# One attention kernel on one core: the two o visits of a burst, run per half of the query columns

## The chip, the cores and the metric

The kernel runs on one core of one Trainium2 chip. The metric is the device time of one execution in microseconds (us), the median of three runs; lower is better. Engines are named as the profile names them: PE is TensorE's matmuls, PEld its weight loads, DVE is VectorE, ACT is ScalarE, POOL is GpSimd, SP is the queue that issues the DMAs. A bank is one of the eight PSUM banks, 512 fp32 columns on 128 partitions.

## The reference

```
x = A_x                                          # 1 x 2048 x 640
g = sigmoid((x * gate_w).sum(-1, keepdims=True))
q = x @ wq  (32 heads of 20)   k = x @ wk   v = x @ wv   (one k and v for all heads)
a = softmax(q k^T * 20 ** -0.5) v @ wo
h = layernorm(B_x)                               # 1 x 2048 x 640
b = (w2^T gelu(w1^T h + b1) + b2)                # the MLP runs over the 2048 tokens, 1728 hidden
out = g * a + (1 - g) * b
```

Attention over 2048 queries and keys for 32 heads, an MLP over the token axis, and a gate that mixes the two.

## The kernel before, in words

The attention is cut into 32 blocks `n` (4 blocks of 512 queries by 8 groups of 4 heads), and each block into 16 units of 128 keys: 512 units. Four kinds of work meet on TensorE, and from about 190 us on they are interleaved in 248 **stretches** of one form (the loop `for j in range(n_st)`):

- **S** (L689, in `qk`): scores of one head for 128 keys by 512 queries, into a bank of 512 columns. ACT reads the bank, takes the exponential and writes a tile `p` (L701); here and there one ACT instruction serves two neighbouring banks (1024 columns).
- **M** (L507, in `ms_next`): the same scores the other way round, only for the row maxima of later blocks. DVE reduces the bank (L515).
- **F** (L839 in the MLP2 stretches; L1014 and L967 before and after them): a step of the MLP or of the output projection, 320 columns, accumulated in a bank `g` of its own.
- **o visits** (L724, in `pv_mm`): `p` times `v` for the four heads of a unit, four fp32 matmuls with 32 output rows each, side by side in the four column groups of the array. Each such matmul is two records in the trace, each with a weight load.

S, M and F matmuls use one half of the array's rows each (62, 60 or 64 rows), so two lanes run at a time: one lane holds the stretch's eight S and some M, the other holds F with an M at its start and one or more at its end. A stretch ends with a **burst**: the o visits of two units, eight matmuls over all 128 rows, accumulated into one bank. After the burst `collect` lets ACT copy the bank to SBUF (L742 for the first pair of units of a block, into `osum`; L745 for the other pairs, into `part`), and POOL adds `part` to `osum` (L746).

S, M and bursts share seven banks (the eighth is `g`). The order of all instructions is fixed while the program is built, by a planner that keeps its own estimate of when each bank is free (`free`), when ACT and DVE are done (`clock`) and how far each lane is (`lane`). A new matmul takes the bank that the planner expects to be free first (`next_free`), and waits on the chip for the engine that last read that bank (`touch`). So a burst waits for a bank, as an S or an M does.

The stretches differ by the F work in them. Those with more than 22 F steps are the MLP's first layer (MLP1, 72 stretches), those with 15 belong to the output projection (48), and the 128 between them are the second layer, **MLP2**. In MLP2 each output tile half has 41 F steps in one lane half and 40 in the other, cut into two batches each, so that of four stretches in a row three have 20 F steps and one has 21. The MLP2 stretches run from about 613.5 to 1330.2 us.

Names and lines of the steps: `burst` holds `next_free`, the call of `pv_mm` for both units and `collect`; L724 is the burst's matmul, L742 and L745 its copy, L746 the sum on POOL, L701 the exponential, L515 the reduction.

Of the kernel before, what the change touches and what calls it, by code (L numbers as in the profile page):

```python
# [10 lines left out]
F32 = mybir.dt.float32  # L11
F32R = mybir.dt.float32r
AF = mybir.ActivationFunctionType
# [5 lines left out]
P = 128  # L19
S, D, H, DH, F = 2048, 640, 32, 20, 1728  # L20
NS = S // P
# [4 lines left out]
NB = 512  # L26
# [13 lines left out]
def mix_kernel(ctx: ExitStack, tc: tile.TileContext, A_x, A_wq, A_wk, A_wv, A_wo,  # L40
               B_x, B_w1, B_b1, B_w2, B_b2, gate_w, out):
    nc = tc.nc
    x = A_x[0]
    y_out = out[0]

    def f32(ap):
        return ap.bitcast(F32)
# [12 lines left out]
    v_sb = const.tile([P, NS, 32], F32, name="v_sb")  # L60
# [392 lines left out]
    p_all = pp_pool.tile([P, 16 * NB], F32, name="p")  # L453
    ev = ctx.enter_context(tc.tile_pool(name="ev", bufs=1))
    copies = ctx.enter_context(tc.tile_pool(name="copies", bufs=2))
    sums = ctx.enter_context(tc.tile_pool(name="sums", bufs=2))
# [8 lines left out]
    def touch(ins, reads=(), writes=(), also=()):  # L465
        need = list(also)
        for r in reads:
            need.append(writer[r])
            readers.setdefault(r, []).append(ins)
        for w in writes:  # L470
            need += readers.pop(w, [])
            writer[w] = ins
        for n in {n.ins.name: n for n in need}.values():
            tc.add_manual_dep(ins.ins, n.ins.name, SYNC, reason="a bank or a p region used again")
        me = str(ins.ins.engine)
        engines.add(me)
        for e in engines - {me}:
            tc.declare_no_dep(ins.ins, group=e, keep=[n.ins for n in need], reason="other banks and p regions")
        tc.add_to_no_dep_group(me, ins.ins)

    def bank(i):
        return span(i, 1) if i < 7 else xs[2]

    def span(i, n):
        t, at = (xs[0], i) if i < 3 else (xs[1], i - 3)
        return t[:, at * NB:(at + n) * NB]
# [121 lines left out]
    with tc.tile_pool(name="psb", bufs=2, space=PSUM, side="right") as psb, \  # L608
# [4 lines left out]
        at, skip, last = 0, 3, NS * PRO - 6  # L613
# [8 lines left out]
        for fc in range(PRO):  # L622
            pu = [psb.tile([P, NB], F32, name=f"pu{r}") for r in range(2)]
            for hf in range(4):
# [4 lines left out]
                for c in range(HS):  # L629
                    st = hf * HS + c  # L630
                    for k, (w, h) in enumerate(((wh, h_hi[0]), (wh, h_lo[0]), (wl, h_hi[0]))):
                        for r in range(2):
                            rows = slice(64 * r, 64 * r + 64)
                            nc.tensor.matmul(pu[r][:, :HD2], w[rows, c, :], h[rows, st, :],  # L634
                                             start=(st == 0 and k == 0), stop=(st == NS - 1 and k == 2))
# [42 lines left out]
    units = [(n, kb) for n in range(NU) for kb in range(NS)]  # L678
    ptiles = {}
    last = {"half": None, "ins": None, "sig": None}  # L680
    flag = const.tile([1, 1], F32, name="flag")

    p_free, p_left = list(range(4)), {}
# [32 lines left out]
    osum = {}  # L716
    later = []

    arrived = []

    def pv_mm(u, o, first, last, i):
        for hh in range(4):
            j = ptiles.pop((u, hh))
            mm = nc.tensor.matmul(o[32 * hh:32 * hh + 32, :], v_sb[:, units[u][1], :], p_all[:, j * NB:(j + 1) * NB],  # L724
                                  start=first, stop=last, skip_group_check=True)
            touch(mm, [("p", j)], [("x", i)], [arrived.pop(0)] if arrived else [])
            p_left[j // 4] -= 1
            if not p_left[j // 4]:
                p_free.append(j // 4)

    def put_o(n, t):
        qb, g = divmod(n, NQ)
        for j in range(2):
            for hh in range(4):
                r = (4 * g + hh) * DH
                nc.sync.dma_start(out=o_scr[j, r:r + DH, qb * NB:(qb + 1) * NB], in_=f32(t[j][32 * hh:32 * hh + DH, :]))

    def collect(u, o, i):
        n, kb = units[u]
        if kb == 1:  # L740
            osum[n] = sums.tile([P, NB], F32, name="osum")
            touch(nc.scalar.activation(osum[n], o, AF.Copy), [("x", i)])  # L742
        else:
            part = copies.tile([P, NB], F32, name="part")
            touch(nc.scalar.activation(part, o, AF.Copy), [("x", i)])  # L745
            nc.gpsimd.tensor_add(osum[n], osum[n], part)  # L746
        if kb == NS - 1:
            later.extend(norm_steps(n))

    def norm_steps(n):  # L750
        t = osum[n]
        ls = ev.tile([P, NB // 32], F32, name="ls")
        rb = ev.tile([P, NB], F32, name="rb")
        hi, lo = rb.bitcast(F32R), t.bitcast(F32R)

        def rows_out():
            nc.sync.dma_start(out=l_scr[n], in_=t.rearrange("(h r) q -> h r q", r=32)[:, DH, :])

        def rows_in():
            nc.sync.dma_start(out=ls, in_=l_scr[n].rearrange("h (c e) -> (h c) e", e=NB // 32))  # L760

        def inverse():
            nc.vector.reciprocal(ls, ls)

        def inverse_out():
            nc.sync.dma_start(out=r_scr[n].rearrange("h (c e) -> (h c) e", e=NB // 32), in_=ls)

        def inverse_in():
            for hh in range(4):
                nc.sync.dma_start(out=rb[32 * hh:32 * hh + 32, :], in_=r_scr[n][hh:hh + 1, :].to_broadcast([32, NB]))  # L770

        def scale():
            nc.gpsimd.tensor_mul(t, t, rb)

        def split():
            nc.gpsimd.tensor_copy(hi, t)
            nc.gpsimd.tensor_sub(lo, t, f32(hi))

        return rows_out, rows_in, inverse, inverse_out, inverse_in, scale, split, lambda: put_o(n, (hi, lo))
# [269 lines left out]
    ph = [(rows[1 - b], rest if b else [], done if b else []) for rows, rest, done in seq for b in range(2)]  # L1049
# [24 lines left out]
    X_US, F_US, O_US = 0.2345, 0.1468, 0.869  # L1074
    W_US, FIRST_US, LAST_US, NEXT_US, SEEN_US = 0.11, 0.1, 0.333, 0.13, 0.43
# [3 lines left out]
    lane, fresh, free = [0.0, 0.0], [True, True], [0.0] * 3 + [1.3] * 4  # L1079
    state = {"at": 0.0, "f": 0.0, "last": 0.0}  # L1080
    reduces = []

    def spend(e, us, at=0.0):
        clock[e] = max(clock[e], at) + us
        return clock[e]

    def next_free():
        return min(range(len(free)), key=lambda i: free[i])
# [99 lines left out]
        while reduces:  # L1188
            reduces.pop(0)[2]()

    def burst(us):
        i = next_free()
        t = max(max(lane) + FIRST_US, state["last"] + LAST_US, free[i]) + len(us) * O_US
        o = bank(i)
        if len(wants) > us[1] // 2 + 2:
            counts = share(us[1] // 2 + 2)
            n = max((given[b] + counts[b] - 1) // 32 for b in range(2))
            if n in qtiles:
                arrived.extend(q_loads.pop(n, ()))
        for u in us:  # L1200
            pv_mm(u, o, u == us[0], u == us[-1], i)
            fetch_at(u)
        collect(us[-1], o, i)
        each, hold = EACH["act"]
        free[i] = spend("act", each, t + 0.25) - each + hold
        lane[:] = [t + NEXT_US] * 2
        fresh[:] = [True, True]

# [8 lines left out]
    def fetch_at(u):  # L1217
        n, kb = units[u]
        if kb == 11 and n + 1 < NU:
            fetch_max(n + 1)  # L1220
# [7 lines left out]
    at = m + 2 * 2 * 2 * NS  # L1228
    left, n = 64 * NU - sum(given) - sum(wants[:at]), n_st - 3 - at
# [12 lines left out]
    for j in range(n_st):  # L1242
        h, i = j % 2, j // 2
        due, stores[:] = stores[:], []
        blocks = [], []
        ss = [lambda at, u=u, pr=pr: qk(u, pr, h, at, blocks[u % 4 // 2], pairs.get(2 * (u % 4) + pr, 1))
              for u in range(4 * i, 4 * i + 4) for pr in range(2)]
        fs, rest, done = ph[j]
        counts, before = share(j), sum(given)
        ms = [[f for f in (ms_next(x) for _ in range(counts[x])) if f] for x in (h, 1 - h)]  # L1250
        owed = sum(counts) - (sum(given) - before)
        pop_chain()
        arrange(h, ss, *ms, fs, done)
        if j % 8 == 7:
            u = j // 8
            for n in (u + 3, u + 4) if u == 0 else (u + 4, u + 5) if u == 1 else (u + 5,):
                if n != 29:
                    new_q(n)
        for f in due:
            f()  # L1260
        if follow:
            follow.pop(0)()
            if len(row_max) == NU and follow:
                follow.pop(0)()
                stores.pop()()
        if not follow and not (j + 1 < n_st and len(ph[j + 1][0]) == 20):
            n = len(row_max)
            follow += ms_done()
            if follow:
                follow.pop(0)()  # L1270
                follow.append(lambda n=n: store_max(n))
        settle()
        pop_chain()
        w1_load(fetched[0] + 3)
        for f in rest:
            f()
        spend("dve", 0.03)
        spend("act", 0.1)
        if j == 8 * 25 - 1:
            new_q(29)  # L1280
        if j:
            burst((2 * j - 2, 2 * j - 1))
        if j == n_st - 2:
            raw = last_wo()

# [146 lines left out]
    for st, d in held:  # L1432
        oT, _ = room(st)
        for j, w in ((0, wo_hi), (1, wo_hi), (0, wo_lo)):
            a, new = acc_at(st, d)
            touch(nc.tensor.matmul(bank(a)[:, :HD2], oT[:, j, 3, :], w[:, 3, d * HD2:(d + 1) * HD2],
                                   start=new, stop=False), writes=[("x", a)])
# [33 lines left out]
```

## Time and profile before

| what | before |
|---|---|
| three timed runs | 1611.63, 1611.82, 1612.45 us; median 1611.82 us |
| profiled execution | span 1610.9 us, the only time that the page gives of it; 0.9 us below the median of the runs |
| PE, PEld | 1602.7 us (99%), 1118.5 us (69%) |
| DVE, ACT, POOL | 1379.7 us (86%), 1261.7 us (78%), 845.4 us (52%) |
| granted TensorE clock | 1.000 of full speed over the span |
| copy of a burst, L745 | 216 of 128x512, mean 601 ns |
| o matmuls, L724 | 4096 records, mean 598 ns |

How to read it: a row of a group gives line, engine, operation, the tile that is written and the one that is read, its shape, how often it ran, the busy time and the mean of one in ns, and then the engine's idle time just before these instructions and who ended it. In a timeline each row is a run of like instructions, with its start, the time from its first start to its last end, and a count; idle time before it and the releaser stand in brackets. A matmul's end is modelled, and matmuls overlap, so a PE that is busy all the time can still be waiting: starts tell more than busy time.

### The profile page before, as it was taken

How to read it: one execution, taken by the hardware profiler on the slowest of the kernel's cores; microseconds unless marked ns; L12 is line 12 of the kernel's file. 1: busy time of each engine (PE TensorE's matmuls, PEld its weight loads, DVE VectorE, ACT ScalarE, POOL GpSimd, SP SyncE). 2: the span in 40 equal slices, each digit the busy share in tenths (PEclk: the TensorE clock that was granted, in tenths of full speed). 3: DMA queues.
4: the chain of work that ended last, by engine and by line, in shares of the span. 5: the costliest groups of instructions: out<-in, count | busy, mean ns of one | idle time of the engine just before them, and what ended most of it. 6: DMA issues, size and time to landing. Idle time of an engine off the chain costs nothing.

```text
span 1610.9 us, 39433 instructions
## 1 busy us (share of the span) xinstructions
PE 1602.7 (99%) x14859; PEld 1118.5 (69%) x14859; DVE 1379.7 (86%) x2626; ACT 1261.7 (78%) x2353; POOL 845.4 (52%) x930
## 2 busy tenths in 40 slices
PE   9999999999999999999999999999999999999998
PEld 7899867767767766666666666666666666666665
DVE  6689899999999999888988989888898986667743
ACT  4445677778778778888888888888888889999996
POOL 6567767777777776544554344444444333333340
PEclk9999999999999999999999999999999999999999
DMA  7665322222222122222211121122211113322341
GB/s 214 205 172 139 93 60 71 65 75 76 69 69 75 49 75 63 81 69 69 59 56 58 38 61 57 54 60 61 61 55 48 46 48 98 118 84 82 89 137 58
DMA packets 180437, 129.53 MB, mean 80 GB/s; under 512 B 41617, under 2 KB 150062, under 8 KB 180246
## 3 DMA queue, kind: packets, MB, share of 16 engines
q1 hardware_dynamic: 179958, 126.68, 27.7%
q8 instruction: 117, 1.92, 0.5%
q14 instruction: 74, 0.61, 0.1%
q10 hardware_dynamic: 288, 0.33, 0.1%
HBM read 93.57 MB, written 32.15 MB: 78 GB/s over the span
## 4 chain that ended last, share of the span: by engine, by line
PE 98%; DMA 1%; DVE 0%; POOL 0%; issue 0%; SPq 0%; ACT 0%; DVEq 0%; POOLq 0%
PE xs L724 30%; PE xs L689 18%; PE xs L507 18%; PE g L839 11%; PE g L1014 7%; PE pu L634 4%; PE pp L303 3%; PE g L967 3%; PE xs L921 1%; PE pp L367 0%; PE x L507 0%; DMA xa<-in_A_x_dram 0%; DMA q_scr<-ql 0%; PE g L507 0%; PE pt L295 0%; PE pp L192 0%
## 5 line engine op out<-in xcount | busy, mean ns | idle before, releaser
L515 DVE TENSOR_REDUCE mp<-xs 128x1 f32<-128x512 f32 x1946 | 1197.9, 684 | 146.5 <-PE xs L689 77.5
L701 ACT ACTIVATE p<-xs 128x512 f32<-128x512 f32 (+1 forms) x1841 | 1014.9, 682 | 3.5 <-PE xs L689 3.4
L746 POOL TENSOR_TENSOR osum<-osum,part 128x512 f32<-128x512 f32 x216 | 279.4, 1294 | 615.3 <-ACT part L745 602.7
L724 PE MATMUL xs<-p,v_sb 128*32 128x512 f32 x4096 | 492.3, 598 | 0.0
L689 PE MATMUL xs<-q,kst 62*128 62x512 f32 x1344 | 477.2, 418 | 1.3 <-ACT p L701 1.3
L507 PE MATMUL xs<-kst,q 60*128 60x512 f32 x1242 | 433.1, 416 | 0.0
L689 PEld LDWEIGHTS xs<-q,kst 62*128 62x128 f32 x1344 | 236.8, 185 | 74.3 <-DVE mp L515 53.9
L745 ACT ACTIVATE part<-xs 128x512 f32<-128x512 f32 x216 | 129.9, 601 | 199.7 <-PE xs L724 198.4
L1014 PE MATMUL g<-slot,w 64*128 64x320 f32 x1728 | 266.8, 306 | 0.0
L724 PEld LDWEIGHTS xs<-p,v_sb 128*32 128x32 f32 x4096 | 107.1, 109 | 226.6 <-issue 157.4
L1014 PEld LDWEIGHTS g<-slot,w 64*128 64x128 f32 x1728 | 259.1, 184 | 2.0
L507 PEld LDWEIGHTS xs<-kst,q 60*128 60x128 f32 x1242 | 207.3, 185 | 72.4 <-DVE mp L515 52.0
L127 POOL TENSOR_TENSOR w<-wr,w 128x512 fp32r<-128x512 f32 (+1 forms) x180 | 225.8, 1256 | 34.3 <-ACT w L124 18.6
L689 PE MATMUL xs<-slot,kst 62*128 62x512 f32 x569 | 207.6, 418 | 0.0
L507 PE MATMUL xs<-kst,slot 60*128 60x512 f32 x576 | 204.2, 418 | 0.0
L839 PE MATMUL g<-u,w 64*128 64x320 f32 x1296 | 201.7, 306 | 0.0
L839 PE MATMUL g<-slot,w 64*128 64x320 f32 x1296 | 201.4, 306 | 0.0
L839 PEld LDWEIGHTS g<-u,w 64*128 64x128 f32 x1296 | 195.7, 184 | 1.7
L839 PEld LDWEIGHTS g<-slot,w 64*128 64x128 f32 x1296 | 195.6, 184 | 1.5
L689 PEld LDWEIGHTS xs<-slot,kst 62*128 62x128 f32 x569 | 100.1, 185 | 30.3 <-DVE mp L515 21.8
L507 PEld LDWEIGHTS xs<-kst,slot 60*128 60x128 f32 x576 | 95.2, 185 | 33.5 <-DVE mp L515 25.2
L967 PE MATMUL g<-slot 64*128 64x320 f32 x720 | 118.2, 307 | 0.0
(189 smaller groups left out, 1449.2 us busy)
## 6 DMA issues: line engine op xcount, KB each, us to landing
wr<-in_B_w_dram SPq DMA_DIRECT2D x155, 256.0 KB
q<-q_scr SPq DMA_DIRECT2D x126, 80.0 KB
rb<-r_scr SPq DMA_DIRECT2D x120, 64.0 KB
slot<-o_scr SPq DMA_DIRECT2D x24, 320.0 KB
y_scr<-yo SPq DMA_DIRECT2D x16, 320.0 KB
q_scr<-qh SPq DMA_DIRECT2D x19, 256.0 KB
q_scr<-ql SPq DMA_DIRECT2D x19, 256.0 KB
o_scr<-rb SPq DMA_DIRECT2D x120, 40.0 KB
```

Source lines behind the costliest of these rows:

```text
L127: nc.gpsimd.tensor_sub(wl, wr, f32(wh))
L507: mm = nc.tensor.matmul(ms, qtiles[n][64 * b:64 * b + 60, pr, qt * P:(qt + 1) * P], kst[64 * b:64 * b + 60, kq * NB:(kq + 1) * NB], start= ...
L515: red = nc.vector.tensor_reduce(out, ms, axis=AX.X, op=ALU.max)
L634: nc.tensor.matmul(pu[r][:, :HD2], w[rows, c, :], h[rows, st, :], start=(st == 0 and k == 0), stop=(st == NS - 1 and k == 2))
L689: mm = nc.tensor.matmul(s, kst[64 * b:64 * b + 62, kb * P:(kb + 1) * P], q[64 * b:64 * b + 62, pr, :], start=True, stop=True)
L701: act = nc.scalar.activation(p_all[:, a * NB:(j + 1) * NB], s, AF.Exp, scale=SCALE)
L724: mm = nc.tensor.matmul(o[32 * hh:32 * hh + 32, :], v_sb[:, units[u][1], :], p_all[:, j * NB:(j + 1) * NB], start=first, stop=last, skip_g ...
L745: touch(nc.scalar.activation(part, o, AF.Copy), [("x", i)])
L746: nc.gpsimd.tensor_add(osum[n], osum[n], part)
L839: other_tile(half, nc.tensor.matmul(hold["p"][:, :HD2], w[r, fc % HS, :], u[d][r, fc, :], start=(hold["n"] == 1), stop=(hold["n"] == 6 * F ...
L967: other_tile(half, nc.tensor.matmul(hold["p"][:, :HD2], o[r, c, :], w[r, c, d * HD2:(d + 1) * HD2], start=(hold["n"] == 1), stop=(hold["n" ...
L1014: other_tile(half, nc.tensor.matmul(hold["p"][:, :HD2], w[r, st % HS, :], h[d][r, st, :], start=(hold["n"] == 1), stop=(hold["n"] == 6 * NS)))
```

## The change

In the MLP2 stretches (those with 16 to 22 F steps) the burst is cut in two by query columns. First both units' visits run for columns 0 to 255, into one bank, and ACT copies these 256 columns; then both units' visits run for columns 256 to 511 into a second bank, and ACT copies those. Both copies go into the two halves of one SBUF tile, and POOL adds the whole tile once, as before. The planner's account of bank and ACT times is made for each half. All other stretches keep the burst as it was. Lines from 720 on move by 1 to 10 (L724 is now L725, both copies are L749, L839 is L845).

```diff
-    def pv_mm(u, o, first, last, i):
+    def pv_mm(u, o, first, last, i, at=0, to=NB):
         for hh in range(4):
-            j = ptiles.pop((u, hh))
-            mm = nc.tensor.matmul(o[32 * hh:32 * hh + 32, :], v_sb[:, units[u][1], :], p_all[:, j * NB:(j + 1) * NB],
-                                  start=first, stop=last, skip_group_check=True)
+            j = ptiles[u, hh]
+            mm = nc.tensor.matmul(o[32 * hh:32 * hh + 32, at:to], v_sb[:, units[u][1], :],
+                                  p_all[:, j * NB + at:j * NB + to], start=first, stop=last, skip_group_check=True)
...
-    def collect(u, o, i):
+    def collect(u, o, i, at=0, to=NB):
         n, kb = units[u]
...
+        t = osum[n] if kb == 1 else parted[0]
+        touch(nc.scalar.activation(t[:, at:to], o[:, at:to], AF.Copy), [("x", i)])
+        if to == NB:
+            if kb > 1:
+                nc.gpsimd.tensor_add(osum[n], osum[n], t)
...
-    def burst(us):
-        i = next_free()
-        t = max(max(lane) + FIRST_US, state["last"] + LAST_US, free[i]) + len(us) * O_US
-        o = bank(i)
+    def burst(us, cuts=(0, NB)):
+        t = max(max(lane) + FIRST_US, state["last"] + LAST_US)
...
-        for u in us:
-            pv_mm(u, o, u == us[0], u == us[-1], i)
-            fetch_at(u)
-        collect(us[-1], o, i)
         each, hold = EACH["act"]
-        free[i] = spend("act", each, t + 0.25) - each + hold
+        for at, to in zip(cuts, cuts[1:]):
+            i = next_free()
+            t = max(t, free[i]) + len(us) * O_US * (to - at) / NB
+            o = bank(i)
+            for u in us:
+                pv_mm(u, o, u == us[0], u == us[-1], i, at, to)
+                if to == NB:
+                    fetch_at(u)
+            collect(us[-1], o, i, at, to)
+            took = each * (to - at) / NB + 0.05 * (to - at < NB)
+            free[i] = spend("act", took, t + 0.25) + hold - each
         lane[:] = [t + NEXT_US] * 2
...
-            burst((2 * j - 2, 2 * j - 1))
+            burst((2 * j - 2, 2 * j - 1), (0, NB // 2, NB) if 15 < len(ph[j][0]) <= 22 else (0, NB))
```

Apart from the split itself the order is the same on every engine: the same sequence of S, M, F and bursts on PE, of reductions on DVE, of exponentials and copies on ACT, and nothing changes on POOL or in the DMA queue. What changes is which bank an instruction gets, and so whom it waits for. TensorE around one burst of MLP2 (in the trace of before it starts at 809.15 us), before; `xs` are the shared banks, and a wait for Activation or DVE is a wait for the last reader of the bank:

```order
L507 MATMUL xs_2761<-kst,q 128x512 [waits Activation_49]
L507 MATMUL xs_2761<-kst,q 128x512 [waits DVE_49]
L724 MATMUL xs_2757<-p,v_sb 32x512 [waits Activation_49]
L724 MATMUL xs_2757<-p,v_sb 32x512 x7
L507 MATMUL xs_2757<-kst,q 128x512 [waits DVE_49]
L689 MATMUL xs_2757<-q,kst 128x512 [waits Activation_49]
L839 MATMUL g<-u_1159,w_91 128x320 [waits DVE_49]
```

TensorE at the same burst in the changed kernel:

```order
L507 MATMUL xs_2761<-kst,q 128x512 [waits Activation_49]
L507 MATMUL xs_2757<-kst,q 128x512 [waits DVE_49]
L725 MATMUL xs_2757<-p,v_sb 32x256 [waits Activation_49]
L725 MATMUL xs_2757<-p,v_sb 32x256 x7
L725 MATMUL xs_2761<-p,v_sb 32x256 [waits DVE_49]
L725 MATMUL xs_2761<-p,v_sb 32x256 x7
L507 MATMUL xs_2761<-kst,q 128x512 [waits Activation_49]
L689 MATMUL xs_2761<-q,kst 128x512 [waits DVE_49]
```

The first half still begins with a wait for an exponential's bank. The second half takes the bank that the next M took before, one that DVE frees, and the matmuls behind it take the next banks in turn. ACT around a burst's copy, before (the two 128x512 rows ahead of the copy are exponentials of the stretch, the three behind it those of the next):

```order
L701 ACTIVATE p<-xs_2757 128x512
L701 ACTIVATE p<-xs_2761 128x512
L745 ACTIVATE part<-xs_2761 128x512
L701 ACTIVATE p<-xs_2757 128x512
L701 ACTIVATE p<-xs_2761 128x1024
L701 ACTIVATE p<-xs_2761 128x512
```

ACT around such a copy in the changed kernel:

```order
L701 ACTIVATE p<-xs_2757 128x512
L749 ACTIVATE part<-xs_2757 128x256
L749 ACTIVATE part<-xs_2761 128x256
L701 ACTIVATE p<-xs_2761 128x512
L701 ACTIVATE p<-xs_2757 128x1024
L701 ACTIVATE p<-xs_2757 128x512
```

One copy of 512 columns has become two of 256 at the same place among the exponentials.

More of the change, by code (lines that the diff above doesn't have):

```diff
@@ L719, in mix_kernel @@
     arrived = []
-    def pv_mm(u, o, first, last, i):
+    parted = [None]
+    def pv_mm(u, o, first, last, i, at=0, to=NB):
         for hh in range(4):
-            j = ptiles.pop((u, hh))
-            mm = nc.tensor.matmul(o[32 * hh:32 * hh + 32, :], v_sb[:, units[u][1], :], p_all[:, j * NB:(j + 1) * NB],
-                                  start=first, stop=last, skip_group_check=True)
+            j = ptiles[u, hh]
+            mm = nc.tensor.matmul(o[32 * hh:32 * hh + 32, at:to], v_sb[:, units[u][1], :],
+                                  p_all[:, j * NB + at:j * NB + to], start=first, stop=last, skip_group_check=True)
             touch(mm, [("p", j)], [("x", i)], [arrived.pop(0)] if arrived else [])
-            p_left[j // 4] -= 1
-            if not p_left[j // 4]:
-                p_free.append(j // 4)
+            if to == NB:
+                del ptiles[u, hh]
+                p_left[j // 4] -= 1
+                if not p_left[j // 4]:
+                    p_free.append(j // 4)
     def put_o(n, t):
@@ L736, in put_o @@
                 nc.sync.dma_start(out=o_scr[j, r:r + DH, qb * NB:(qb + 1) * NB], in_=f32(t[j][32 * hh:32 * hh + DH, :]))
-    def collect(u, o, i):
+    def collect(u, o, i, at=0, to=NB):
         n, kb = units[u]
[L740 to L748, printed above, removed]
+        if at == 0:
+            if kb == 1:
+                osum[n] = sums.tile([P, NB], F32, name="osum")
+            else:
+                parted[0] = copies.tile([P, NB], F32, name="part")
+        t = osum[n] if kb == 1 else parted[0]
[3 more added lines that the diff above has]
+                nc.gpsimd.tensor_add(osum[n], osum[n], t)
+            if kb == NS - 1:
+                later.extend(norm_steps(n))
     def norm_steps(n):
@@ L1199, in burst @@
                 arrived.extend(q_loads.pop(n, ()))
-        for u in us:
-            pv_mm(u, o, u == us[0], u == us[-1], i)
-            fetch_at(u)
-        collect(us[-1], o, i)
         each, hold = EACH["act"]
-        free[i] = spend("act", each, t + 0.25) - each + hold
+        for at, to in zip(cuts, cuts[1:]):
[4 more added lines that the diff above has]
+                pv_mm(u, o, u == us[0], u == us[-1], i, at, to)
+                if to == NB:
+                    fetch_at(u)
+            collect(us[-1], o, i, at, to)
+            took = each * (to - at) / NB + 0.05 * (to - at < NB)
+            free[i] = spend("act", took, t + 0.25) + hold - each
         lane[:] = [t + NEXT_US] * 2
```

## The prediction

> **What bounds the kernel now.** I read the page first, then the waits of the MLP2 window, then timelines of single stretches. The page says that TensorE is the chain that ends last:
>
> ```profile
> PE 1602.7 (99%) x14859; PEld 1118.5 (69%) x14859; DVE 1379.7 (86%) x2626; ACT 1261.7 (78%) x2353; POOL 845.4 (52%) x930
> PE 98%; DMA 1%; DVE 0%; POOL 0%; issue 0%; SPq 0%; ACT 0%; DVEq 0%; POOLq 0%
> ```
>
> That alone would say that nothing off PE matters. But matmul ends are modelled and overlap, so a short wait between two matmuls does not show as idle PE. The weight loads show it. Of the waits of PEld in the MLP2 window (613.5 to 1330.2 us), by line, releaser, total, count and longest, this is the one of the bursts:
>
> ```profile
> PEld xs L724 <- ACT p L701: 38.1, 128, 0.3
> ```
>
> Every one of the 128 bursts of MLP2 starts when ACT ends an exponential: the burst needs a bank, and its bank is the one that this exponential reads. Part of each 0.3 us is there anyway, since the array runs empty between the lanes and the burst. The size of the rest comes from the starts. Four ends of stretches on PE: a stretch with 20 F steps at 809 us, one with 21 that ends at 814 us, one with 20 near the end of MLP2, and one of the later stage:
>
> ```profile
> 808.71 0.46 PE L507 MATMUL xs<-kst,q 60*128 60x512 f32 x2
> 809.15 1.92 PE L724 MATMUL xs<-p,v_sb 128*32 128x512 f32 x16
> 811.00 0.50 PE L507 MATMUL xs<-kst,q 60*128 60x512 f32 x1
> 811.01 0.50 PE L689 MATMUL xs<-q,kst 62*128 62x512 f32 x1
> ...
> 814.50 0.40 PE L507 MATMUL xs<-kst,q 60*128 60x512 f32 x1
> 814.83 1.92 PE L724 MATMUL xs<-p,v_sb 128*32 128x512 f32 x16
> ...
> 1324.12 0.46 PE L507 MATMUL xs<-kst,q 60*128 60x512 f32 x2
> 1324.56 0.64 PE L724 MATMUL xs<-p,v_sb 128*32 128x512 f32 x4
> ...
> 1343.77 0.39 PE L689 MATMUL xs<-q,kst 62*128 62x512 f32 x1
> 1344.09 0.64 PE L724 MATMUL xs<-p,v_sb 128*32 128x512 f32 x4
> ```
>
> From the last matmul's start to the burst's start it is 0.33 us (814.50 to 814.83) and 0.32 (1343.77 to 1344.09) where the lanes decide, but 0.44 (808.71 to 809.15, and 1324.12 to 1324.56) at the ends of the 20-step stretches. So these lose 0.44 - 0.33 = 0.11 us each, waiting for ACT. The 21-step stretches, one in four, have one F step more in the lane that ends last and lose nothing: 96 stretches lose 0.11, that is 10.6 us in all. This is the most that an earlier ACT can give here.
>
> Why is ACT late at that point? Its own timeline from one burst to the next:
>
> ```profile
> 806.12 3.96 ACT L701 ACTIVATE p<-xs 128x512 f32<-128x512 f32 x7
> 811.20 0.60 ACT L745 ACTIVATE part<-xs 128x512 f32<-128x512 f32 x1 [1.12 <-PE xs L724]
> 811.70 0.59 ACT L701 ACTIVATE p<-xs 128x512 f32<-128x512 f32 x1
> ```
>
> ACT runs its seven exponential instructions without a gap (one row of 3.96 us), then idles 1.12 us until the burst ends, copies for 0.60 us, and only then begins the next chain. The burst waits for the fifth of the seven:
>
> ```profile
> 808.45 0.65 ACT L701 ACTIVATE p<-xs 128x512 f32<-128x512 f32 x1
> ```
>
> It ends at 809.10 and the burst starts at 809.15. So in 20-step stretches the loop is: burst, copy, five exponentials back to back, burst. TensorE only fills it.
>
> **The change part by part.** *The copy.* The first half's copy falls into ACT's 1.12 us of idle time while the second half still runs; its cost on ACT is hidden there. The second half's copy stands where the whole one stood, but is shorter. The nearest ACT copy of 256 columns is in the prologue, the whole one beside it:
>
> ```profile
> L390 ACT ACTIVATE wq_hi<-wr 128x256 fp32r<-128x256 f32 x5 | 1.9, 409 | 0.3 <-DMA wr<-in_A_wq_dram 0.2
> L745 ACT ACTIVATE part<-xs 128x512 f32<-128x512 f32 x216 | 129.9, 601 | 199.7 <-PE xs L724 198.4
> ```
>
> That is 0.41 against 0.60 us, 0.19 less. The next exponential overlaps the copy's end by 0.10 (copy ends 811.80, exponential starts 811.70), so ACT could take it at 811.20 + 0.41 - 0.10 = 811.51. Its scores are there at 811.01 + 0.50 = 811.51, and an engine begins about 0.04 after a matmul's end, as DVE does here with the M that ended at 811.50:
>
> ```profile
> 811.54 0.69 DVE L515 TENSOR_REDUCE mp<-xs 128x1 f32<-128x512 f32 x1 [0.45 <-PE xs L689]
> ```
>
> So the chain begins at 811.55 instead of 811.70: 0.15 us earlier, now bound by data and no longer by the copy. As the chain has no gap, its fifth member ends 0.15 earlier too, and the burst could begin at 809.15 - 0.15 = 809.00. The lanes allow 809.15 - 0.11 = 809.04. Late next are the lanes, by 0.04 us, and the whole 0.11 comes back.
>
> *The second bank.* The second half waits for a bank that DVE frees. Reductions around the burst:
>
> ```profile
> 808.48 1.29 DVE L515 TENSOR_REDUCE mp<-xs 128x1 f32<-128x512 f32 x2
> 809.69 1.28 DVE L515 TENSOR_REDUCE mp<-xs 128x1 f32<-128x512 f32 x2
> ```
>
> The first reduction of the upper row ends close to the burst's start, about half the row (0.6 us) ahead of the second's end at 809.77; moved by 0.11 it ends about 0.1 us into the burst. The second half begins halfway, 0.9 us in: the bank has been free for 0.8 us. Queued behind this wait on PE are the second half and then all of the next stretch; if the next reduction were meant, 0.7 us in, it would still be free. Behind it each S and M takes a bank that comes free one step later in turn, and two banks come back from copies instead of one: the first some 0.9 us earlier than the one bank does now, the second 0.19 earlier. No matmul of the next stretch waits longer for that. Cost nothing.
>
> *The matmuls.* Sixteen matmuls of 256 columns replace eight of 512: 64 records with loads instead of 32, and the columns in sum stay the same, so the burst can't become shorter. Loads in the burst:
>
> ```profile
> 809.15 0.16 PEld L724 LDWEIGHTS xs<-p,v_sb 128*32 128x32 f32 x8 [0.30 <-ACT p L701]
> 809.61 0.13 PEld L724 LDWEIGHTS xs<-p,v_sb 128*32 128x32 f32 x4 [0.30 <-issue]
> 810.03 0.13 PEld L724 LDWEIGHTS xs<-p,v_sb 128*32 128x32 f32 x4 [0.30 <-issue]
> ```
>
> The burst goes in sets of four (one per column group). Loads for two sets go in at once, then those of the third as the second begins (809.61), and those of the fourth as the third begins (810.03): one set lasts 0.42 us, and a load of 0.13 us lies under it. A half set lasts 0.21, still longer than 0.13, so the loads stay hidden with 0.08 to spare. What a set costs beside its columns doesn't show at the rows' 0.01 us: an added set costs between 0 and 0.01, and I take 0.005, four added sets 0.02 us a burst, 128 x 0.02 = 2.6 us.
>
> A rule speaks against this. The Trainium skill, "TensorE: Matmul & The Clock Gate", section "The mechanism" (row and column tiling), says that a weight load runs beside matmuls in flight only where it goes to another row group. The burst's matmuls all use the same 128 rows, so by that rule each load lies bare. The three rows above disagree: loads start 0.42 us before their matmuls. It is a rival below.
>
> *POOL and the rest.* The sum on POOL begins when the second copy ends, 0.19 earlier than now. The DMA queue and DVE's order are as before.
>
> **Sum.** -96 x 0.11 = -10.6, matmuls +2.6: -8.0 us. The profiled execution's span 1610.9 would become 1602.9, and the median, 0.9 above it, 1611.8 - 8.0 = 1603.8.
>
> **The rivals.** *Records set the burst's pace* (slower). The burst has 64 loads and matmuls to issue in 1.85 us, 29 ns each. The densest long stretch of this trace is the MLP's first part:
>
> ```profile
> 96.60:150.00 53.40, 53.40 (x689) 52.25 (x690) 49.07 (x89) 24.86 (x48) 38.03 (x33) 1.00 0.60 167
> ```
>
> 1379 records in 53.4 us, 39 ns each. If that were the engine's limit, a burst would take 64 x 0.039 = 2.48 us, 0.63 more: +81 us, less at most 10.6, about 1682. It decides from 10.6 / 128 = 0.083 us a burst on, a pace of 30 ns a record. For it: nothing in the trace runs denser for long. Against: at 809.15 eight loads start within 0.05 us (0.16 less one load's 0.11), so prepared records go out quickly, and there is a whole stretch to prepare them in. Chance 0.05.
>
> *Loads lie bare* (slower). With 0.13 us for each of the four added sets the burst takes 0.52 more: 128 x 0.52 - 10.6 = +56 us, about 1668. Against it are the load rows. Chance 0.04.
>
> *The gain comes in part.* The 0.15 is only 0.04 above need. Were a half copy from a bank dearer, or the first exponential later, so that 0.06 us comes through, it is -96 x 0.06 + 2.6 = -3.2: 1608.6. Chance 0.10.
>
> *Nothing is gained*: another wait ends the stretch at the same time, so that the burst is again held to 0.44 us, by the seven shared banks, of which a burst now takes two. Then only the matmuls' cost is left, 1611.8 + 2.6 = 1614.4. For it: DVE is as tight as ACT, idle only 0.45 us at the stretch's head. Chance 0.08.
>
> **How the numbers follow.** The forecast has 0.73, the partial gain 0.10, no gain 0.08, the two slow cases 0.09. The range: lowest is the whole 10.6 at no cost, 1601.2, rounded down to 1601.0; the forecast with 0.01 per added set is 1606.3; the partial gain reaches 1608.6, rounded to 1609.0. That leaves out 0.17. A measurement of this kernel can tell about 0.2%, 3.2 us, from no change. Faster by more: the forecast and some 0.06 of the partial case, 0.79. Within: the rest of that and no gain, 0.12. Slower: 0.09.
>
> **What would show it.** Right: in 20-step stretches the last matmul's start to the burst's start falls from 0.44 to 0.32 or 0.33; in 21-step stretches it stays; the first exponential starts about 0.55 us after the first S instead of 0.69; burst start to next S stays at 1.85 to 1.89; one copy of about 0.41 lies in the idle time before the burst's end. Wrong: a burst of over 1.93 us, sets of clearly more than 0.21 us or a gap at the half; or a burst that still waits 0.44 us, with DVE as its releaser.

## The result, and the profile after

| | before | changed |
|---|---|---|
| median of four runs | 1611.72 us | 1599.67 us (1599.25 to 1599.84) |
| ratio, 95% interval | | 0.9923 [0.9909, 0.9937] |
| span of the profiled execution | 1610.9 us | 1597.9 us |

The change is faster by 12.05 us. The forecast was 8.0, with 1601.0 as the lowest time of the range: sign and stage were right, the size was not.

Nearly all of it lies in MLP2. The window from its first to its last burst, of before and then of the changed kernel (start and end, length, then busy time and instructions of PE, PEld, DVE, ACT and POOL, then clock and DMA):

```profile
613.51:1330.22 716.71, 716.71 (x6691) 480.94 (x6689) 643.31 (x1203) 586.08 (x1058) 329.92 (x358) 1.00 0.20 58
```

```profile
613.32:1317.97 704.65, 704.65 (x8723) 547.21 (x8721) 643.29 (x1203) 619.62 (x1185) 330.81 (x358) 1.00 0.21 60
```

716.71 - 704.65 = 12.06, of the 13.0 us between the two profiled executions. PE is shown as busy all the time in both, with some 2000 records more in the shorter one: its busy time says nothing of these waits.

PE at a burst of the changed kernel. It stands behind a 20-step stretch (805.99), the next one behind a 21-step stretch (811.60):

```profile
805.65 0.41 PE L507 MATMUL xs<-kst,q 60*128 60x512 f32 x2
805.99 1.93 PE L725 MATMUL xs<-p,v_sb 128*32 128x256 f32 x32
807.86 0.50 PE L507 MATMUL xs<-kst,q 60*128 60x512 f32 x1
807.86 0.49 PE L689 MATMUL xs<-q,kst 62*128 62x512 f32 x1
...
811.29 0.39 PE L507 MATMUL xs<-kst,q 60*128 60x512 f32 x1
811.60 1.93 PE L725 MATMUL xs<-p,v_sb 128*32 128x256 f32 x32
```

At the end of the 20-step stretch the distance from the last M to the burst is 0.34 us where it was 0.44 (medians of the 96: 0.33 and 0.43). At the end of the 21-step stretch it is 0.31 where it was 0.33, but the medians of the 32 are 0.33 and 0.32: nothing is gained at that place, so that a gain of these stretches must be looked for further up. The burst lasts 807.86 - 805.99 = 1.87 to the next matmul, against 1.85.

ACT between the same two bursts, with its two copies:

```profile
807.19 0.38 ACT L749 ACTIVATE part<-xs 128x256 f32<-128x256 f32 x1 [0.31 <-PE xs L725]
807.99 0.39 ACT L749 ACTIVATE part<-xs 128x256 f32<-128x256 f32 x1 [0.42 <-PE xs L725]
808.42 1.52 ACT L701 ACTIVATE p<-xs 128x512 f32<-128x512 f32 x2
```

The first copy lies under the second half, as forecast. The first exponential starts 808.42 - 805.99 = 2.43 us after the burst's start; before it was 811.70 - 809.15 = 2.55. That is 0.11 us earlier, not 0.15. After the next burst (811.60) it is another time:

```profile
813.60 0.38 ACT L749 ACTIVATE part<-xs 128x256 f32<-128x256 f32 x1 [0.42 <-PE xs L725]
814.00 0.60 ACT L701 ACTIVATE p<-xs 128x512 f32<-128x512 f32 x1
```

Here it starts at 814.00 - 811.60 = 2.40, which is 0.15 earlier. Both kinds are frequent; they are counted below.

The mean stretch, from the distances of the burst starts in the two traces:

| | count | before | changed | difference | in all | forecast, net |
|---|---|---|---|---|---|---|
| 20 F steps | 96 | 5.575 us | 5.471 us | -0.104 us | -10.0 us | -8.64 us |
| 21 F steps | 32 | 5.672 us | 5.607 us | -0.065 us | -2.1 us | +0.64 us |

### The profile page after: what moved, and what is told of

Read it like the earlier page. It is cut to its first block, busy times and chain, and to the rows that moved or that the text cites. A ratio compares the mean times of both kernels' runs of the same rounds, so it can differ in the third digit from the quotient of the medians.

```text
span 1597.9 us, 43453 instructions
## 1 busy us (share of the span) xinstructions
PE 1590.6 (100%) x16907; PEld 1184.9 (74%) x16907; DVE 1379.6 (86%) x2626; ACT 1295.5 (81%) x2481; POOL 845.9 (53%) x930
## 4 chain that ended last, share of the span: by engine, by line
PE 99%; POOL 0%; DVE 0%; issue 0%; ACT 0%; DVEq 0%; POOLq 0%
PE xs L725 30%; PE xs L689 18%; PE xs L507 18%; PE g L845 11%; PE g L1020 7%; PE pp L303 4%; PE pu L634 4%; PE g L973 3%; PE x L507 1%; PE xs L927 1%; PE pt L295 0%; PE pp L367 0%; PE pp L192 0%; PE xs L1426 0%; PE g L927 0%; PE xs L1446 0%
## 5 line engine op out<-in xcount | busy, mean ns | idle before, releaser
L725 PE MATMUL xs<-p,v_sb 128*32 128x256 f32 (+1 forms) x6144 | 493.6, 454 | 0.0
L507 PE MATMUL xs<-kst,q 60*128 60x512 f32 x1242 | 426.6, 408 | 0.0
L725 PEld LDWEIGHTS xs<-p,v_sb 128*32 128x32 f32 x6144 | 173.6, 109 | 210.5 <-issue 81.3
L749 ACT ACTIVATE part<-xs 128x256 f32<-128x256 f32 (+1 forms) x328 | 149.1, 455 | 156.8 <-PE xs L725 155.4
L507 PEld LDWEIGHTS xs<-kst,q 60*128 60x128 f32 x1242 | 212.2, 184 | 50.4 <-DVE mp L515 19.3
L845 PE MATMUL g<-u,w 64*128 64x320 f32 x1296 | 200.5, 305 | 0.0
L845 PE MATMUL g<-slot,w 64*128 64x320 f32 x1296 | 200.3, 305 | 0.0
L507 PE MATMUL xs<-kst,slot 60*128 60x512 f32 x576 | 200.1, 407 | 0.0
L845 PEld LDWEIGHTS g<-u,w 64*128 64x128 f32 x1296 | 195.3, 184 | 1.9
L845 PEld LDWEIGHTS g<-slot,w 64*128 64x128 f32 x1296 | 195.1, 184 | 1.5
L973 PEld LDWEIGHTS g<-slot 64*128 64x128 f32 x720 | 111.8, 185 | 4.1 <-DVE mm L537 0.8
```

What stands on the lines that cost most here:

```text
L507: mm = nc.tensor.matmul(ms, qtiles[n][64 * b:64 * b + 60, pr, qt * P:(qt + 1) * P], kst[64 * b:64 * b + 60, kq * NB:(kq + 1) * NB], start= ...
L725: mm = nc.tensor.matmul(o[32 * hh:32 * hh + 32, at:to], v_sb[:, units[u][1], :], p_all[:, j * NB + at:j * NB + to], start=first, stop=last ...
L749: touch(nc.scalar.activation(t[:, at:to], o[:, at:to], AF.Copy), [("x", i)])
L845: other_tile(half, nc.tensor.matmul(hold["p"][:, :HD2], w[r, fc % HS, :], u[d][r, fc, :], start=(hold["n"] == 1), stop=(hold["n"] == 6 * F ...
L973: other_tile(half, nc.tensor.matmul(hold["p"][:, :HD2], o[r, c, :], w[r, c, d * HD2:(d + 1) * HD2], start=(hold["n"] == 1), stop=(hold["n" ...
```

## The experiments

My theory after the result: the whole gain is ACT's earlier chain of exponentials. The edits below are against the changed kernel and are shown in part. The rivals: the second bank brings it, or the halved matmuls do, or the shorter copy alone counts.

**The halves without the copies.**

```diff
+        i = next_free()
+        t = max(t, free[i]) + len(us) * O_US
+        o = bank(i)
         for at, to in zip(cuts, cuts[1:]):
-            i = next_free()
...
             for u in us:
                 pv_mm(u, o, u == us[0], u == us[-1], i, at, to)
...
-            collect(us[-1], o, i, at, to)
...
+        collect(us[-1], o, i)
```

> The matmuls of the MLP2 bursts run per half, as in the change, but both halves go into one bank, and one copy of 512 columns follows, as before. Theory (the gain is ACT's earlier chain: the shorter copy at the burst's end lets the exponentials begin some 0.11 us earlier, and with them the banks come free that bursts and late M wait for): nothing is gained, the split costs 0.010 us a burst (first X 1.864 after the burst's start against 1.854), 128 x 0.010 = +1.3: 1613.0. Rival (the halved matmuls themselves help, by reading p in smaller pieces): as the changed kernel, 1599.7. Rival (a second bank helps): 1613.0 too, so this run does not tell it from the theory.

Measured: 1613.19 us, before 1611.83; ratio 1.0008 [0.9999, 1.0017]. The split of the matmuls gives nothing. In the trace the first matmul follows 1.864 us after the burst's start, against 1.854: the price of the split is 0.010 us.

**The short copy without the halves.**

```diff
...
+            sl = slice(cuts[1], NB)
+            touch(nc.scalar.activation(part[:, sl], o[:, sl], AF.Copy), [("x", i)])
+            nc.gpsimd.tensor_add(osum[n][:, sl], osum[n][:, sl], part[:, sl])
...
```

> Bursts whole and in one bank as before, but in MLP2 ACT copies only columns 256 to 511 of the bank, and POOL adds only these (for the first pair of a block the copy is whole). Left out: the copy and sum of the other 256 columns. Theory (ACT's chain starts earlier): the whole gain without the cost of the split, 1599.7 - 1.3 = 1598.4, between 1597.5 and 1600. Rival (the second bank and the early return of the first one bring the gain): there is one bank only, so at most its return 0.19 us earlier, 1610 to 1612.

Measured: 1601.90 us, ratio 0.9939 [0.9927, 0.9952]. With one bank and whole matmuls, 9.9 us of the gain are there. So the second bank is not its source; but 3.5 us less came than expected. Of these, 16 bursts explain about 1.5 us: they end the first pair of a block, their copy stays whole, and the stretch behind them takes 5.57 us (median) instead of 5.47. ACT after a burst with the short copy (it starts at 805.74):

```profile
807.80 0.39 ACT L1218 ACTIVATE part<-xs 128x256 f32<-128x256 f32 x1 [1.13 <-PE xs L725]
808.17 0.60 ACT L701 ACTIVATE p<-xs 128x512 f32<-128x512 f32 x1
```

The copy starts 807.80 - 805.74 = 2.06 us after the burst's start, while the change's second copy starts at 807.99 - 805.99 = 2.00, although its burst is longer. Something in the change, beside the copy's length, makes the last copy early.

**The first copy after the second half, in words only.**

```diff
+        made = []
...
+            free[i] = float("inf")
...
+            made.append((o, i, at, to))
+        for o, i, at, to in made:
             collect(us[-1], o, i, at, to)
```

> Two halves in two banks as in the change, but both copies stand after the second half, so that the first one is no longer under the matmuls. Theory: two copies take longer on ACT than the one of 512 columns by 0.07 to 0.09 us, so ACT's chain begins later than before: 96 x (0.08 + 0.01) + 32 x 0.02 = +9, about 1621, slower than before. Rival (the second bank): two banks of half the columns come back, the first 0.2 us earlier than the whole one did: most of the gain, 1600 to 1604.

Measured: 1604.84 us, ratio 0.9956 [0.9944, 0.9969]. The expectation fell because the edit doesn't do what I meant. The copies follow each other on ACT in the change as well, and each waits only for its own half's matmuls. What the edit did change is the planner's account: 51 stretches got another order of S, M and F, among them all with 21 steps. The medians of all 20-step and all 21-step stretches are those of the change (5.472 and 5.605 us), but some stretches are longer, so that the means are 5.506 and 5.654. As a test of the theory this run is void; it is repeated below.

**A copy shorter by 64 columns.**

```diff
-            burst((2 * j - 2, 2 * j - 1), (0, NB // 2, NB) if 15 < len(ph[j][0]) <= 22 else (0, NB))
+            burst((2 * j - 2, 2 * j - 1), (0, NB // 8, NB) if 15 < len(ph[j][0]) <= 22 else (0, NB))
```

> As the change, but cut at column 64: the first piece has 64 columns, the second 448. Theory: the copy at the end is shorter by 64 columns, about 0.05 us, so ACT begins 0.05 earlier: 96 x -(0.05 - 0.01) and about 32 x -0.04, together -5: 1606.5. Rival (the second bank): two banks, the first returned even earlier than in the change: all of the gain or more, 1599 to 1600.

Measured: 1600.37 us, ratio 0.9929 [0.9915, 0.9943]. That is what the second bank should give, not what the theory as stated gave. ACT at this kernel's burst (start 806.02):

```profile
806.76 0.30 ACT L749 ACTIVATE part<-xs 128x64 f32<-128x64 f32 x1
808.02 0.55 ACT L749 ACTIVATE part<-xs 128x448 f32<-128x448 f32 x1 [0.96 <-PE xs L725]
808.46 0.59 ACT L701 ACTIVATE p<-xs 128x512 f32<-128x512 f32 x1
```

The copy is 0.05 us shorter (0.55 against 0.60), but it also starts 2.00 us after the burst's start, 0.05 earlier than the whole copy of before. The exponential comes at 2.44: 0.11 early, though half of that was expected. So the same unknown 0.05 as above. The copies' rows in the MLP2 window of before tell what it is (median durations in ns):

```profile
L745 ACT ACTIVATE part<-xs x112: 597/598/600, 615.6 to 1326.6; 128x512 f32<-128x512 f32 x112
L745 ACTq EVENT_SEMAPHORE  x110: 17/17/17, 615.5 to 1326.5; - x110
```

110 of the 112 copies have an instruction ahead of them that only waits. (The Trainium skill, "Perfetto Trace Analysis", section "Identifying Dependency Chains", says that an instruction which waits for several engines may get such instructions put ahead of it; the rows agree.) The copy waits for two engines, TensorE for its data and POOL for the SBUF tile that it overwrites. In the trace the wait for TensorE, the one that ends last, became the instruction of its own, and the copy itself carries the wait for POOL. The 110 copies with this pair start 2.05 us after their burst (median), the two without it 1.99. In the changed kernel the first copy carries the pair; the second, the one at the burst's end, waits for TensorE alone. The next two runs take the second bank and this wait apart.

**The first copy held back.** Order, banks and planner as in the change; only a wait is added.

```diff
...
+        for o, i, at, to in made:
+            collect(us[-1], o, i, at, to, [writer["x", made[-1][1]]])
```

> As the change, in the same order and with the same two banks, but the first half's copy also waits for the second half's matmuls, so that both copies stand between the burst and the next exponential. (The earlier run that should have done this left ACT's order and waits as they are in the change, so it tested nothing of it.) Theory (ACT's chain): first copy 0.20 us after the burst, the second 0.28 behind it, the first exponential another 0.28 behind: 2.62 us after the burst's start instead of 2.54, so 20-step stretches take 5.65 us and 21-step ones about 5.72: 96 x 0.076 + 32 x 0.05 = +9, 1620.6, slower than before. Rival (the second bank brings the gain): the banks are two as in the change, each back about as early as the one was before: 1600 to 1606.

Measured: 1621.81 us, ratio 1.0061 [1.0049, 1.0073]. With two banks as in the change, and the first copy moved from under the matmuls, the gain turns into a loss of the expected size. ACT after a burst that starts at 811.77:

```profile
813.83 0.66 ACT L749 ACTIVATE part<-xs 128x256 f32<-128x256 f32 x2 [1.13 <-PE xs L725]
814.38 0.60 ACT L701 ACTIVATE p<-xs 128x512 f32<-128x512 f32 x1
```

Both copies take 0.66 us, and the exponential begins 2.61 us after the burst's start. The second bank as such is out as a source. An earlier return of a bank is another matter; the next run, with one bank, bears on it.

**One wait for the whole copy.** Nothing is split.

```diff
...
+        if early[0] and kb > 1:
+            nc.scalar.activation(seen_pool, osum[n][:, :1], AF.Copy)
         touch(nc.scalar.activation(t[:, at:to], o[:, at:to], AF.Copy), [("x", i)])
...
```

> Bursts whole, one bank, one copy of 512 columns as before. New is a one-column ACT instruction ahead of each copy of MLP2, in ACT's idle time, that reads the sum on POOL: ACT has then seen POOL's last result, and the copy itself waits for TensorE alone instead of for TensorE and POOL. Theory with what the runs added (a copy with two waits starts 0.06 us later, since one wait is an instruction of its own: 1.989 and 2.051 us in the trace of before; the change's second copy has one wait): ACT's chain begins 0.06 earlier with nothing split: 80 x 0.061 + 32 x 0.055 = -6.6, 1605.1. Rival (only the shorter copy counts): no change, 1611.8.

Measured: 1603.74 us, ratio 0.9949 [0.9936, 0.9961]. A one-column instruction in idle time brings 8.4 us, seven tenths of what the change does, and 1.4 us more than expected. ACT after a burst that starts at 806.66:

```profile
808.65 0.60 ACT L752 ACTIVATE part<-xs 128x512 f32<-128x512 f32 x1 [0.98 <-PE xs L726]
809.14 0.59 ACT L701 ACTIVATE p<-xs 128x512 f32<-128x512 f32 x1
```

The copy is whole (0.60 us) but starts at 1.99 instead of 2.05, and the exponential at 2.48 instead of 2.55. One more rival is that the added instruction helps by shortening ACT's idle time ahead of the copy. It is out: the 16 copies of first pairs (into `osum`) have no such instruction ahead of them, but here they too carry the wait for TensorE themselves, and they too start at 1.99 (15 of the 16 at 2.04 before). The expectation had left these copies out.

**The 21-step stretches.**

```diff
-            burst((2 * j - 2, 2 * j - 1), (0, NB // 2, NB) if 15 < len(ph[j][0]) <= 22 else (0, NB))
+            burst((2 * j - 2, 2 * j - 1), (0, NB // 2, NB) if j + 1 < n_st and len(ph[j + 1][0]) == 21 else (0, NB))
```

> Only the 32 bursts that stand ahead of a stretch with 21 F steps are split, all others are whole. Theory (in 21-step stretches of before, the load of an M waits for an exponential's bank until 5.087 us after the burst, the last F's load is queued behind it at 5.090 instead of 4.98, and this costs some 0.06 us a stretch): 32 x -0.0645 = -2.1 net of the split, 1609.6. Rival (the recorded step that these stretches lose nothing): only the cost, 32 x 0.010 = +0.3, 1612.0.

Measured: 1609.53 us, before 1611.77; ratio 0.9986 [0.9978, 0.9995]. The 32 stretches gain 2.2 us, where the prediction had them lose. Where the time lay is seen in the weight loads of before at the end of such a stretch:

```profile
813.84 0.19 PEld L689 LDWEIGHTS xs<-q,kst 62*128 62x128 f32 x1
813.98 0.18 PEld L839 LDWEIGHTS g<-u,w 64*128 64x128 f32 x1
814.24 0.18 PEld L507 LDWEIGHTS xs<-kst,q 60*128 60x128 f32 x1
814.24 0.18 PEld L839 LDWEIGHTS g<-u,w 64*128 64x128 f32 x1
```

with ACT's exponential

```profile
813.55 0.64 ACT L701 ACTIVATE p<-xs 128x512 f32<-128x512 f32 x1
```

It ends at 814.19; the M at L507 needs its bank and loads at 814.24. The last F step (L839) needs no bank, but stands behind this M in TensorE's order, and its load starts at 814.24 too, 0.26 us after the F before it. The same place of the changed kernel, loads and exponential:

```profile
810.70 0.33 PEld L845 LDWEIGHTS g<-u,w 64*128 64x128 f32 x2
810.97 0.18 PEld L507 LDWEIGHTS xs<-kst,q 60*128 60x128 f32 x1
811.00 0.18 PEld L845 LDWEIGHTS g<-u,w 64*128 64x128 f32 x1
811.14 0.19 PEld L507 LDWEIGHTS xs<-kst,q 60*128 60x128 f32 x1
```

```profile
810.30 0.62 ACT L701 ACTIVATE p<-xs 128x512 f32<-128x512 f32 x1
```

The exponential ends at 810.92, 4.93 us after the stretch's burst (805.99), where it was 814.19 - 809.15 = 5.04; the M loads at 810.97 and the F follows 0.03 later, at its own time. All 32 stretches show it, and in three kernels, in the medians: the M's load comes 0.051 us after that exponential's end (5.034 and 5.085 us after the burst before, 4.974 and 5.025 with one wait for the whole copy, 4.925 and 4.976 in the change), and the last F's load follows the F before it by 0.25, 0.19 and 0.15 us.

**Quarters: do loads or records set the pace?** One bank, one copy, four pieces of 128 columns.

> The MLP2 bursts run per quarter of 128 columns, all into one bank, one copy of 512 columns at the end: sixteen sets of 128 columns. Theory (a load of 0.13 us for four column groups lies under the set before it): a quarter set is 0.107 us, shorter than the load, so the loads now show: sixteen sets of 0.13 instead of 1.72 us, +0.36 us a burst, 128 x 0.36 = +46: about 1658. Rival (loads cost nothing here, a set costs 0.0025 beside its columns): twelve added sets, 0.03 a burst, +3.8: 1615.5. Rival (records set the pace, 39 ns each): 128 records, 5.0 us a burst, +400.

Measured: 1615.64 us, before 1611.77; ratio 1.0024 [1.0014, 1.0033], the time of the first rival to 0.1 us. PE and PEld at a burst:

```profile
809.69 1.95 PE L725 MATMUL xs<-p,v_sb 128*32 128x128 f32 x64
811.57 0.50 PE L507 MATMUL xs<-kst,q 60*128 60x512 f32 x1
```

```profile
809.69 1.69 PEld L725 LDWEIGHTS xs<-p,v_sb 128*32 128x32 f32 x64 [0.30 <-ACT p L701]
811.57 0.18 PEld L507 LDWEIGHTS xs<-kst,q 60*128 60x128 f32 x1 [0.20 <-DVE mp L515]
```

64 loads and 64 matmuls in 811.57 - 809.69 = 1.88 us, 15 ns a record, and only 0.03 us more than the whole burst. That loads would show, as I expected here, was wrong by 42 us.

**A still shorter copy, and other stages.** Cut at column 384:

> As the change, but cut at column 384: the copy at the end has 128 columns instead of 256. Theory: in the change the first exponential begins 0.05 us after the end of the copy and 0.07 after its scores; it is bound by the scores, and the lanes follow close behind, so a still shorter copy gives nothing: 1599.7, within 0.8. Rival (the copy's length still decides): 0.1 us earlier again, down to the lanes' floor of 0.317 us at the end of each stretch, 96 x -0.015 = -1.5 and no more: 1598.2.

Measured: 1599.52 us, ratio 0.9924 [0.9912, 0.9936]: the same as the change, as the theory had it. (20 of the 20-step stretches got another order here.) All bursts split:

> All bursts are split, those of MLP1 and of the output projection too. Theory: there the lanes decide when the burst starts (0.32 to 0.33 us from the last matmul), so that an earlier ACT gives nothing and the split costs 0.010 us each: 120 x 0.010 = +1.2 over the change, 1600.9. Rival (the split helps wherever ACT copies): another 120 x 0.06 to 0.1 less, 1588 to 1593.

Measured: 1602.91 us, ratio 0.9944 [0.9930, 0.9957]. Neither held. The time after MLP2 fell from 279.9 to 278.9 us, but up to MLP2 it rose from 613.3 to 618.0. Splitting moves the planner's estimates, and 42 MLP1 stretches got another order, as did 38 behind MLP2. Some 20 of the 42 end in three M one after the other, which share the seven banks, as on PE here:

```profile
458.24 0.65 PE L507 MATMUL xs<-kst,q 60*128 60x512 f32 x3
458.82 0.42 PE L725 MATMUL xs<-p,v_sb 128*32 128x256 f32 x4
```

0.58 us from the first of them to the burst. How much of the loss is the order and how much the split itself wasn't separated. MLP2 and the projection split, MLP1 whole:

> The bursts of MLP2 and of the output projection are split, those of MLP1 whole. From the run with all bursts split: there the time after MLP2 fell from 279.9 to 278.9 us, and MLP1 lost. If the two stages add, 1599.7 - 1.0 = 1598.7. If the lanes alone decide in the projection (theory as stated for that run), the split costs 48 x 0.010 = +0.5: 1600.2.

Measured: 1598.64 us, before 1612.16; ratio 0.9916 [0.9903, 0.9929]. It is the fastest kernel here; its distance to the change (0.9923) lies inside both intervals, and the time after MLP2 in its trace is 279.0 us against 279.9. The same 38 stretches behind MLP2 have another order in it, so what the split alone does there isn't separated.

## Why the prediction was wrong in size

The median 20-step stretch of each trace, from the starts: end of the fifth exponential instruction after the burst, and start of the next burst, both from the burst's start.

| kernel | fifth exponential ends | next burst |
|---|---|---|
| first copy held back | 5.597 us | 5.650 us |
| quarters, one bank | 5.553 | 5.606 |
| halves, one bank | 5.534 | 5.586 |
| before | 5.523 | 5.576 |
| one wait for the whole copy | 5.464 | 5.516 |
| short copy only | 5.432 | 5.484 |
| cut at 64 | 5.421 | 5.474 |
| the change, 32 stretches that begin with an M | 5.416 | 5.470 |
| cut at 384, the same 32 | 5.416 | 5.470 |
| the change, 64 stretches that begin with an S | 5.383 | 5.468 |
| cut at 384, the same 64 | 5.383 | 5.470 |

The first seven rows keep 0.052 or 0.053 us between the two columns, and the 32 stretches of the change keep 0.053. In the other 64 the burst comes 0.08 later than the exponential, 0.33 from the last M: there the lanes hold it. That is the loop that the prediction named (burst, copy, five exponentials, burst), and the lanes as what is late next. **This step was right**, and the rival that another wait takes over is out.

**The 21-step stretches "lose nothing": wrong, 2.7 us of the 4.05 us missed.** I read the loss only at the stretch's end, where the last matmul stands 0.33 us ahead of the burst, and took that as proof that ACT doesn't matter in these stretches. But the lane's own length held a wait: the last F's load was 0.26 us after the one before, behind an M that waited for the exponential's bank. Forecast +0.64, measured -2.1. The row of 128 waits for ACT didn't tell the two kinds of stretches apart: before, the burst follows the fifth exponential by 0.05 us after 20 steps and by 0.14 after 21.

**The price of the split: half of the forecast.** I took 0.02 us a burst; the first matmul comes 0.010 us later. In the 96 stretches of 20 steps that makes 1.0 of the 1.35 us missed there. The other 0.4 is the term of the wait: 0.104 + 0.010 = 0.114 us came back, where I had read 0.11 from four rows.

**ACT's 0.15 us were reached in half of the stretches.** The chain starts when its scores are there, as forecast. In 64 of the 20-step stretches an S stands first: its exponential starts 0.04 us behind the scores, at 2.40 us after the burst's start (before 2.54), and the lanes decide. In the other 32, and in all with 21 steps, an M stands ahead of the S, as at 807.86: the exponential starts 0.07 behind its scores (807.86 + 0.49 = 808.35, exponential 808.42), at 2.43, and the chain is 0.11 early. Why these start 0.03 later wasn't found. The prediction had read its 0.04 from a start of DVE. In these 32 stretches the margin of 0.04 is gone, and 0.11 is just what the lanes allow: that ACT and the lanes come out at the same 5.47 us is luck.

The half copy took 0.39 us for 0.41 forecast, and it started 0.05 us earlier than the whole one, which the prediction had not seen. In the change the copy no longer decides: cut at 384, it ends another 0.10 us earlier (2.28 against 2.39), and the exponentials start at the same two times. Nor is the early start needed where an M stands first: with the short copy only, the copy starts at 2.05, and the exponentials of these 32 stretches still start at 2.42, after a burst that is 0.01 shorter. (Where an S stands first they start at 2.45 in that run; most of them have a waiting instruction of their own ahead of them there, which those of the change have not.) So the shorter copy and the single wait are two ways to the same thing, an earlier chain, and they don't add up: the scores come next.

**Loads and records**, both slow rivals: out. The run with quarters shows it, and in the changed kernel the second half waits for nothing: the 32 loads of its burst stand in one row of 1.45 us.

```profile
805.99 1.45 PEld L725 LDWEIGHTS xs<-p,v_sb 128*32 128x32 f32 x32 [0.25 <-ACT p L701]
```

## What to carry to other kernels

When banks are shared, the engine that empties them can set the pace of an in-order queue, as ACT did here, even if the profile calls that queue busy for 99% of the span: look at starts and at weight loads, and follow the released wait back to the first instruction of its chain. What counts there is when the chain starts, so put work that must precede it under something else, and see how many waits its first instruction carries. Before writing that a stretch loses nothing, compare the pitch inside it too, not only its end.

## What the runs showed of the hardware

- An ACT copy that waits for two engines, with the wait for TensorE in an instruction of its own ahead of it, started 0.06 us later than one that carries the wait for TensorE itself (2.05 against 1.99 us after the burst's start, whole copy). Taking the second wait away was worth 8.4 us here. What it costs when the earlier wait stands ahead isn't shown.
- Loads of 0.13 us for four column groups stayed hidden even under sets of 128 columns, all on the same 128 rows: 128 records in 1.88 us, 0.03 us more than 32 records. An added set cost 0.0025 us (1.854, 1.864 and 1.884 us for 4, 8 and 16 sets). The rule of the Trainium skill weighed in the prediction ("TensorE: Matmul & The Clock Gate", "The mechanism") doesn't hold for this burst.
- A load that waits for a bank holds up the next load in TensorE's order, though that one goes to the other half of the rows and waits for nothing: 0.25 us (median of 32) between two F loads that are otherwise 0.15 apart.
